# Attention with memory and a gated MoE on one Trainium2 core: the first two blocks as whole float32 stages with z as a column of M, and the first batches' statistics as squares on ACT

## The chip, the cores and the metric

One core of a Trainium2 chip runs the kernel. The metric is device time in microseconds (us), the median of several runs. The kernel before takes 677.45 us (three runs, 676.85 to 678.27).

The engines are named as in the profile: PE (matrix products; PEld is its weight load), DVE (vector), ACT (activations), POOL (GpSimd) and SP, which here only issues DMAs. ACT and POOL can issue DMAs too. Every engine takes its instructions in order.

## The reference

```python
# attention: B, H, S, D = 4, 8, 576, 64
scores = matmul(q, k.T) / sqrt(D), causal
local  = softmax(scores) @ v                 # sum + 1e-9
q_p    = where(q > 0, q, exp(q) - 1) + 1     # phi
mem    = (q_p @ M_prev) / (q_p @ z_prev + 1e-6)
x      = sigmoid(beta) * mem + (1 - sigmoid(beta)) * local
# MoE: 2304 tokens, d_model 512, d_ff 1536, weights float64
xn  = x / sqrt(mean(x * x) + 1e-6) * rms_g
g   = xn @ w_gate
out = (g * sigmoid(g) * (xn @ w_val)) @ w_out
```

## The kernel before

**Blocks and chunks.** The 2304 tokens are 18 blocks of 128 rows, and two blocks make a chunk of 256 tokens, which goes through the MoE together. Blocks 0 and 1 are the first 128 rows of batches 0 and 1. They and chunk 0 are computed in float32. All other blocks split each operand into two float16 parts, a high and a low one, with a power-of-two scale per batch. That scale comes from statistics of the whole batch (the largest norms of k, v and M), so no block after the first two can start before its batch's rows have all been looked at.

**Weights.** They arrive as float64 words in pieces of 512 KB: 24 pieces of `w_gate` and `w_val` (three thirds of eight) and 12 of `w_out`. `f64_to_f32` (L777 to L781) turns a piece into float32 in three steps, one on ACT and two on DVE. Raw pieces lie in a ring of five places in the tile `wo`; a load also waits until the conversion three pieces before it has begun (`PACE`, `paced`). For the later chunks' scales PE forms column sums of the converted pieces (`gram`, L147): four 128x128 products each, whose diagonal bounds the squares.

**Statistics of batches 0 and 1.** `stat_blk` (L232) does the same on the rows of k and v: grams of the four blocks and the tail, tiles `kv` or `pre`, 48 and 32 products. Blocks 2 and 3 of each batch, which are needed in SBUF only later, are loaded for this alone by `load_pre` (L752) into the one buffer of tag `res`, over SP's queue. DVE reduces the sums, with a factor of 1.03. `stat_M` squares M on ACT (`square_acc`, L222).

**Blocks 0 and 1.** k, q and phi(q) are transposed on PE and copied out of PSUM by DVE (L355). Scores, exponentials (L474 on ACT), transposed probabilities, products with v and M go in units of four heads. The sum q_p @ z is a matmul with one column per head (`zn`, L558). M of both batches lies in places of `wo`. The result is squared (L225), its norm is formed on POOL, and a product with a diagonal (L691) gives `xT0`, chunk 0's input. Chunk 0's twelve projections F0 to F11 (L851, float32, sixteen records each) then need all pieces of their third, and its output products (L911) the pieces of `w_out`.

**Order.** The program is a list of steps with estimated lengths and priorities (`PRIO`); a scheduler that simulates the engines lays them into one order per engine. Order on SP's queue matters most, since a load that waits holds up all that stand behind it.

```python
raws[p] = hold(p, 2 * (p % NR))                                        # L746
ins = nc.sync.dma_start(out=raws[p].bitcast(I64), in_=w[...])          # L747
begun[p] = nc.scalar.activation(dst, r[:, :, 1], AF.Prelu, ...)        # L777
nc.vector.tensor_scalar(ri[:, :, 0], ri[:, :, 0], 29, ...)             # L778
nc.vector.scalar_tensor_tensor(out=di, in0=di, scalar=3, ...)          # L779
```

Of the kernel before, what the change touches and what calls it, by code (L numbers as in the profile page):

```python
# [30 lines left out]
ADD32 = "p"  # L31
DIAG = True
T32 = "ddddd"
# [17 lines left out]
RING = 5  # L51
# [7 lines left out]
def attn_memory_moe_kernel(  # L59
# [134 lines left out]
    pre, held = {}, {}  # L194
# [12 lines left out]
    def load_M(b):  # L207
        if b < 2:
            held["M", b, 0] = held["M", b, 1] = NF - b + 100
            qst[("M", b)] = wo[:, NF - b, :]  # L210
        else:
            qst[("M", b)] = sb.tile([P, HD], F32, tag="q", name=f"M{b}")
        for hf in range(2):
            nc.sync.dma_start(
                out=qst[("M", b)][hf * D : (hf + 1) * D], in_=M_prev[b].rearrange("d h e -> d (h e)")
            )
# [5 lines left out]
    def square_acc(src, acc):  # L222
        junk = sb.tile([P, HD], BF16, tag="junk", name="junk", bufs=1)
        np_ = src.shape[0]
        nc.scalar.activation(junk[:np_, : src.shape[1]], src, AF.Square, accum_out=acc)  # L225
# [6 lines left out]
    def stat_blk(b, i):  # L232
        if b < 2:
            r = slice(0, P) if i < NI else slice(b * TR, b * TR + TR)
            src = pre.pop((b, i)) if (b, i) in pre else stage[blk_of[(b, i)] if i < NI else NI * 2]
            for j in range(2):
                if i == 0:
                    csum["kv", b, j] = ps.tile([P, 512], F32, tag="out", name=f"csum{j}")
                gram(csum["kv", b, j], src[r, j], i == 0, i == NI)
                if i == NI:  # L240
                    nc.vector.tensor_reduce(
                        stt[b][:, j, 0:1], csum.pop(("kv", b, j))[:, :P], axis=AX.X, op=ALU.max
                    )
            return
# [9 lines left out]
    def stat_M(b):  # L254
# [6 lines left out]
        del held["M", b, 0]  # L261

    def stat_end(b):
# [6 lines left out]
        if b < 2:  # L270
            nc.vector.tensor_scalar(mx[:, :2], over_partitions(mx[:, :2], 2), 1.03, None, op0=ALU.mult)
            pow2_scales(mx[:, :2], 2, c[:, 0:2], c[:, 3:5])
# [14 lines left out]
    def prep_M(b):  # L287
        src = (qst.pop if b >= 2 else qst.get)(("M", b)).rearrange("p (h e) -> p h e", h=H)
# [23 lines left out]
    def q_stats(n):  # L312
        ss = tiny.tile([P, 2], F32, tag="ss", name="ss")
# [81 lines left out]

    def u_scores(n, h0):
        b, i = blocks[n]
        G = group(n)
        tag = "P16" if n < NA and h0 // G % 2 else "S"
        s = sb.tile([P, NI * P + P], F32, tag=tag, name="S")  # L400
# [5 lines left out]
        for g in range(G):  # L406
            h = h0 + g
            if n < NA:
                h, r = head32(h)
                for j in range(i + 1):  # L410
                    nc.tensor.matmul(
                        t[:, g * w + j * P : g * w + (j + 1) * P], q32[n][r, 0, h // 2, :],
                        k32[blk_of[(b, j)]][r, h // 2, :], start=True, stop=True,
                    )
            elif i < NI:
# [7 lines left out]
        for g in range(G):  # L423
            nc.vector.tensor_tensor_reduce(  # L424
                out=s[:, g * w : (g + 1) * w], in0=t[:, g * w : (g + 1) * w],
                in1=mask[:, m0 : m0 + w], scale=qsc[n][:, 5:6] if n >= NA else -1.0 / float(D) ** 0.5,
# [4 lines left out]
        if n >= NA:  # L431
            nc.vector.tensor_scalar(nm0, nm0, LNP, None, op0=ALU.add)  # L432
# [33 lines left out]
    def u_exp(n, h0):  # L466
        s, w, nm = Ssb[(n, h0)]
        G = group(n)
        if n < NA:
            if h0 % 4 == 0:  # L470
                den[n, h0 // 4] = tiny.tile([P, 2, 4], F32, tag="qsc", name="den", bufs=5)
            for g in range(G):
                v_ = s[:, g * w : (g + 1) * w]
                nc.scalar.activation(  # L474
                    v_, v_, AF.Exp, bias=nm[:, g : g + 1], scale=-1.0,
                    accum_out=den[n, h0 // 4][:, 1, (h0 + g) % 4 : (h0 + g) % 4 + 1],
                )
            Ssb[(n, h0)] = s
            return
# [789 lines left out]
```

## Time and profile before

| what | before |
|---|---|
| median of 3 runs | 677.45 us (676.85 to 678.27) |
| profiled execution, its span | 677.3 us |
| instructions | 16070 |
| PE busy | 623.5 us (92%) |
| PEld busy | 489.4 us (72%) |
| DVE busy | 474.8 us (70%) |
| ACT busy | 384.1 us (57%) |
| POOL busy | 164.3 us (24%) |
| mean granted TensorE clock | 0.944 of full speed |
| moved by DMA | 88.63 MB, 131 GB/s in the mean |

The profiled execution's own time is its span, 677.3 us. A share of busy time is a mean over the whole span; the stages at the start have other limits than the rest, and the rows further down are of those stages. The granted clock is the speed that PE was given, 1.00 being 2.4 GHz and 0.50 being 1.2 GHz.

### The profile page before, as it was taken

What the parts mean: (1) busy time and instruction counts of PE and PEld (TensorE: products, weight loads), DVE (VectorE), ACT (ScalarE), POOL (GpSimd) and SP (SyncE); (2) the same over time, 40 slices, a digit from 0 to 9 for tenths busy, and PEclk for the clock granted to TensorE, in tenths of its full rate; (3) what the DMA queues carried; (4) which work ended last, traced back from release to release, by engine and by line L of the source; (5) the groups of instructions that cost most, each with busy time, mean ns of one, the idle gap of its engine ahead of it and who ended that gap; (6) DMA issues with size and microseconds to landing.
All of it is one profiled execution on the core that took longest, in us unless ns stands there. A gap on an engine that the chain in (4) does not pass through costs nothing.

```text
span 677.3 us, 16070 instructions
## 1 busy us (share of the span) xinstructions
PE 623.5 (92%) x6152; PEld 489.4 (72%) x6152; DVE 474.8 (70%) x1448; ACT 384.1 (57%) x799; POOL 164.3 (24%) x239
## 2 busy tenths in 40 slices
PE   5898968899798969999899899989999999999997
PEld 4786857755686647778687777767787788887774
DVE  5556977897899776689668666877887676872221
ACT  3334655647778776665657656956557554542322
POOL 0001110131255324232143122522232221212111
PEclk9655988899999969999899999999999999999999
DMA  7745899933933777636466763285785454351001
GB/s 257 271 165 198 253 273 249 208 72 63 226 76 76 170 161 167 142 76 146 112 139 111 167 161 64 51 153 135 124 135 114 90 93 99 76 76 21 32 1 31
DMA packets 191660, 88.63 MB, mean 131 GB/s; under 512 B 174176, under 2 KB 174176, under 8 KB 191584
## 3 DMA queue, kind: packets, MB, share of 16 engines
q1 hardware_dynamic: 191136, 87.59, 56.2%
q8 instruction: 48, 0.79, 0.5%
q14 instruction: 28, 0.23, 0.1%
q10 hardware_dynamic: 448, 0.02, 0.0%
HBM read 36.20 MB, written 4.72 MB: 60 GB/s over the span
## 4 chain that ended last, share of the span: by engine, by line
PE 56%; DMA 19%; DVE 11%; ACT 7%; issue 4%; SPq 2%; POOL 1%; ACTq 0%; DVEq 0%; POOLq 0%
PE gv L858 26%; DMA PT<-P 6%; PE out L920 4%; PE out L921 4%; PE out L919 4%; DMA wo<-in_moe_w_out_dram 3%; DMA kv<-in_qkv_dram 3%; PE sc L418 3%; PE sc L445 2%; ACT junk L225 2%; DVE S L424 2%; DMA wo<-in_moe_w_gate_dram 2%; DMA qT<-row 2%; DVE P L500 1%; DMA wo<-in_moe_w_val_dram 1%
## 5 line engine op out<-in xcount | busy, mean ns | idle before, releaser
L858 PE MATMUL gv<-xT,wgv 128*128 128x256 f16 x2304 | 314.5, 274 | 1.3 <-DMA xT<-x 1.3
L858 PEld LDWEIGHTS <-wgv 128*128 128x128 f16 x2304 | 221.9, 98 | 38.4 <-DMA xT<-x 1.5
L890 POOL TENSOR_TENSOR h<-th,h 128x256 f16<-128x256 f32 x96 | 72.4, 754 | 263.1 <-ACT h L889 202.8
L482 ACT ACTIVATE S<-S,nm 128x256 f32<-128x256 f32 (+4 forms) x128 | 75.1, 608 | 47.9 <-DVE nm L432 34.6
L418 PE MATMUL sc<-kT,qT 128*128 128x128 f16 x608 | 84.1, 221 | 4.5 <-DMA qT<-qT 1.8
L500 DVE TENSOR_TENSOR P<-S,P 128x512 f16<-128x512 f32 (+2 forms) x84 | 64.6, 769 | 26.3 <-ACT P L487 25.7
L874 ACT ACTIVATE th<-gv,wt 128x256 f32<-128x256 f32 x96 | 44.8, 467 | 57.4 <-PE gv L858 53.4
L875 DVE SCALAR_TENSOR_TENSOR th<-th,gv 128x256 f32<-128x256 f32 x96 | 39.9, 415 | 52.7 <-ACT th L874 52.1
L424 DVE CUSTOM_DVE_ANT_0 S<-sc,mask,qsc 128x256 f32<-128x256 f32 (+3 forms) x112 | 62.2, 573 | 17.6 <-PE sc L418 14.1
L920 PE MATMUL out<-wo,h 128*128 128x512 f16 x192 | 73.2, 382 | 0.4 <-DVE wo L98 0.4
L921 PE MATMUL out<-wo,h 128*128 128x512 f16 x192 | 72.3, 381 | 0.0
L919 PE MATMUL out<-wo,h 128*128 128x512 f16 x192 | 72.1, 382 | 0.0
L487 ACT CAST P<-S 128x512 f16<-128x512 f32 (+2 forms) x100 | 59.6, 596 | 12.1 <-DMA PT<-P 10.8
L526 PE MATMUL loc<-v,PT 128*128 128x65 f16 x304 | 50.2, 195 | 14.3 <-DMA PT<-P 14.1
L889 ACT CAST h<-th 128x256 f16<-128x256 f32 x96 | 38.4, 400 | 43.9 <-DVE th L878 42.0
L418 PEld LDWEIGHTS <-qT 128*128 128x128 f16 x608 | 51.2, 98 | 10.6 <-issue 3.4
L851 PE MATMUL gv<-xT,wgv 128*128 128x256 f32 x192 | 47.8, 405 | 6.0 <-DVE h32e L878 6.0
L527 PE MATMUL loc<-v,PT 128*128 128x64 f16 x304 | 50.0, 195 | 0.0
L528 PE MATMUL loc<-v,PT 128*128 128x65 f16 x304 | 50.0, 195 | 0.0
L878 DVE SCALAR_TENSOR_TENSOR th<-th,wt,gv 128x256 f32<-128x256 f32 x96 | 45.8, 477 | 1.7
L660 POOL TENSOR_TENSOR t<-t,t 128x256 f32<-128x256 f32 x32 | 25.8, 806 | 86.0 <-DVE t L656 73.5
L851 PEld LDWEIGHTS gv<-xT,wgv 128*128 128x128 f32 x192 | 37.7, 202 | 12.3 <-DVE h32e L878 6.4
(216 smaller groups left out, 1141.5 us busy)
## 6 DMA issues: line engine op xcount, KB each, us to landing
kv<-in_qkv_dram SPq DMA_DIRECT2D x36, 256.0 KB, 3.6
wo<-in_moe_w_gate_dram SPq DMA_DIRECT2D x12, 512.0 KB, 5.5
wo<-in_moe_w_val_dram SPq DMA_DIRECT2D x12, 512.0 KB, 5.3
q<-in_qkv_dram SPq DMA_DIRECT2D x18, 256.0 KB, 3.0
wo<-in_moe_w_out_dram SPq DMA_DIRECT2D x8, 512.0 KB, 4.6
qT<-qT SPq DMA_DIRECT2D x32, 128.0 KB, 2.4
out_dram<-res SPq DMA_DIRECT2D x16, 256.0 KB, 2.3
pre<-in_qkv_dram SPq DMA_DIRECT2D x8, 256.0 KB, 3.0
```

Of the source, the lines that this page charges most:

```text
L418: nc.tensor.matmul(t[:, g * w + j * P : g * w + (j + 1) * P], qT[n][:, t2, h, :], kT[blk_of[(b, j)]][:, h, :], start=(t2 == 0), stop=(t2 = ...
L424: nc.vector.tensor_tensor_reduce(out=s[:, g * w : (g + 1) * w], in0=t[:, g * w : (g + 1) * w], in1=mask[:, m0 : m0 + w], scale=qsc[n][:, 5 ...
L482: nc.scalar.activation(v_, v_, AF.Exp, bias=nm[:, g : g + 1], scale=-1.0)
L487: nc.scalar.copy(p16[:, : G * w], s[:, : G * w])
L500: eng.tensor_tensor(p16[:, w : 2 * w], s[:, :w], p16[:, :w], ALU.subtract)
L526: nc.tensor.matmul(a, phi_, vhi, start=(j == 0), stop=False)
L851: nc.tensor.matmul(o, wgv[:, 1 + p, o0 : o0 + P], xT[0][:, cc, :], start=(cc == 0), stop=(cc == NC - 1))
L858: nc.tensor.matmul(o, lhs, xT[c][:, rhs, :], start=(cnt == 0), stop=(cnt == 3 * NC - 1))
L890: nc.gpsimd.tensor_tensor(h16[:, 1], th, h16[:, 0], ALU.subtract)
L919: nc.tensor.matmul(o, hh, whi, start=(f == 0), stop=False)
L920: nc.tensor.matmul(o, hh, wlo, start=False, stop=False)
L921: nc.tensor.matmul(o, hl, whi, start=False, stop=(f == NF - 1))
```

## The change

1. Blocks 0 and 1 are written as whole stages `scores32`, `mem32`, `pv32` and `evac32`, ahead of the list of steps and at high priority, each over all eight heads. M of batches 0 and 1 lies in tiles `Mz` of tag `v16`, with z as a 65th column, so that one product per head gives both; the `zn` products go. Of ten PSUM copies per pair (`T32`) four go to ACT; the addition of the two halves (`ADD32`) goes from POOL to DVE.
2. The statistics of batches 0 and 1 are squares on ACT (20 of up to 512 columns). The grams on `kv` and `pre`, their reductions and the factor 1.03 go. The eight `pre` loads are issued on POOL's queue (`PREQ`), each into a place of its own of tag `v16`.
3. The ring of raw pieces has six places in place of five; `kv2`, `kv3` and the tail's `kv` are loaded in one row after block 1's inputs; z's scale is a step of its own, `setup_z`.

```diff
-ADD32 = "p"
+ADD32 = "d"
-T32 = "ddddd"
+T32 = "dadda"
-RING = 5
+RING = 6
+PREQ = "p"
...
     def load_M(b):
         if b < 2:
-            held["M", b, 0] = held["M", b, 1] = NF - b + 100
-            qst[("M", b)] = wo[:, NF - b, :]
+            t = sb.tile([P, H, VW], F16, tag="v16", name=f"Mz{b}", bufs=10)
+            Mz[b] = t.bitcast(F32)
+            qst[("M", b)] = Mz[b][:, :, :D]
...
+        if b < 2:
+            nc.gpsimd.tensor_copy(Mz[b][:, :, D], zz[:, b * H : (b + 1) * H])
...
     def stat_blk(b, i):
-        if b < 2:
-            r = slice(0, P) if i < NI else slice(b * TR, b * TR + TR)
-            src = pre.pop((b, i)) if (b, i) in pre else stage[blk_of[(b, i)] if i < NI else NI * 2]
-            for j in range(2):
-                if i == 0:
-                    csum["kv", b, j] = ps.tile([P, 512], F32, tag="out", name=f"csum{j}")
-                gram(csum["kv", b, j], src[r, j], i == 0, i == NI)
...
+        if (b, i) in pre:
+            for j, src in enumerate(pre.pop((b, i))):
+                square_acc(src, stt[b][:, j, i : i + 1])
             return
...
+    def mem32(n):
+        b = blocks[n][0]
+        accs[n] = [ps.tile([P, 4, D + 1], F32, tag="out", name=f"mem{n}_{u}") for u in range(2)]
+        for g in range(4):
+            for u in range(2):
+                h, r = head32(4 * u + g)
+                nc.tensor.matmul(
+                    accs[n][u][:, g], q32[n][r, 1, h // 2, :], Mz[b][r, h, :], start=True, stop=True
+                )
...
-    def mem32(n, g4):
-        b, i = blocks[n]
-        if g4 == 0:
-            z = ps.tile([P, 2, 4], F32, tag="sc", name="zn")
-            for x in range(H):
-                h, r = head32(x)
...
-                nc.tensor.matmul(
-                    zt[:, x // 4, x % 4 : x % 4 + 1], q32[n][r, 1, h // 2, :],
-                    zz[r, b * H + h : b * H + h + 1], start=True, stop=True,
-                )
...
     def load_pre(b, i):
-        pre[(b, i)] = sb.tile([P, 2, HD], F32, tag="res", name=f"pre{b}_{i}", bufs=1)
+        pre[(b, i)] = []
         for j in range(2):
-            nc.sync.dma_start(out=pre[(b, i)][:, j], in_=qkv[blk_of[(b, i)], :, j, :])
+            t = sb.tile([P, H, VW], F16, tag="v16", name=f"pre{b}_{i}_{j}", bufs=10)
+            t = t.bitcast(F32).rearrange("p a b -> p (a b)")[:, :HD]
+            PRE.dma_start(out=t, in_=qkv[blk_of[(b, i)], :, j, :])
+            pre[(b, i)].append(t)
...
-    load_kv(2), load_kv(3)
     setup_consts()
-    for n in range(2):
-        prep_qk32(n)
-        phi_calc(n)
-        prep_phi32(n)
+    with tc.high_priority(PRIO[0]):
+        for n in range(2):
+            prep_qk32(n)
+            phi_calc(n)
+            scores32(n)
+            prep_phi32(n)
+            mem32(n)
+        for n in range(2):
+            pv32(n)
+            evac32(n)
+            x_norm(n)
+            x_float(n)
     load_q(2)
+    load_kv(2), load_kv(3), load_kv(2 * NI)
+    for i in range(2, NI):
+        for b in range(2):
+            load_pre(b, i)
+    with tc.high_priority(PRIO[0]):
+        setup_z()
```

What that does to the order of instructions stands below at three places. A row is line, operation, out<-in and shape; `x4` is four such in a row, and the numbers in names count tiles.

On SP's queue, after the inputs of block 1, the kernel before has

```order
L220 DMA q2_188<-in_qkv_dram 128x512
L747 DMA wo_84<-in_moe_w_gate_dram 128x512
L747 DMA wo_84<-in_moe_w_val_dram 128x512
L220 DMA q3_766<-in_qkv_dram 128x512
L747 DMA wo_84<-in_moe_w_val_dram 128x512
L756 DMA pre0_3_529<-in_qkv_dram 128x512 x2
L747 DMA wo_84<-in_moe_w_val_dram 128x512 x2
L747 DMA wo_84<-in_moe_w_gate_dram 128x512
L756 DMA pre1_2_635<-in_qkv_dram 128x512 x2
L747 DMA wo_84<-in_moe_w_gate_dram 128x512 x3
L756 DMA pre1_3_646<-in_qkv_dram 128x512 x2
L747 DMA wo_84<-in_moe_w_val_dram 128x512 x4
```

and the changed kernel, whose weight loads are at L739,

```order
L224 DMA q2_343<-in_qkv_dram 128x512
L206 DMA kv2_345<-in_qkv_dram 128x512 x2
L206 DMA kv3_348<-in_qkv_dram 128x512 x2
L206 DMA kv8_351<-in_qkv_dram 128x512 x2
L739 DMA wo_84<-in_moe_w_gate_dram 128x512
L739 DMA wo_84<-in_moe_w_val_dram 128x512
L224 DMA q3_603<-in_qkv_dram 128x512
L739 DMA wo_84<-in_moe_w_val_dram 128x512 x3
L739 DMA wo_84<-in_moe_w_gate_dram 128x512 x4
L739 DMA wo_84<-in_moe_w_val_dram 128x512 x4
L739 DMA wo_84<-in_moe_w_gate_dram 128x512 x4
L739 DMA wo_84<-in_moe_w_val_dram 128x512 x3
```

The `pre` loads are gone from among the weight loads; `kv2`, `kv3` and the tail `kv8` stand ahead of the fourth weight piece.

On ACT, from the square of block 0's result (`t1_0`; `wgv<-wo` is a conversion, `ph` a step of phi, `ssm` belongs to M's statistics, `ss` to q's), the kernel before has

```order
L225 ACTIVATE junk_326,xs_325<-t1_0_289 128x512
L777 ACTIVATE wgv_83<-wo_84 128x512 x5
L225 ACTIVATE junk_388,xs_387<-t1_1_374 128x512
L335 ACTIVATE ph_738<-q2_188 128x512
L777 ACTIVATE wgv_83<-wo_84 128x512
L225 ACTIVATE junk_471,ssm0_470<-wo_84 128x512
L777 ACTIVATE wgv_83<-wo_84 128x512 x2
L225 ACTIVATE junk_594,ssm1_593<-wo_84 128x512
L225 ACTIVATE junk_709,ss_708<-q2_188 128x512
L777 ACTIVATE wgv_83<-wo_84 128x512
```

and the changed kernel, from the square of block 1's result, with `stt` for the statistics of k and v and conversions at L771,

```order
L233 ACTIVATE junk_331,xs_330<-t1_1_324 128x512
L233 ACTIVATE junk_371,zq_370<-zz_86 128x32
L771 ACTIVATE wgv_83<-wo_84 128x512 x2
L233 ACTIVATE junk_466,ssm0_465<-Mz0_101 128x512
L233 ACTIVATE junk_492,stt0_490<-kv0_98 128x512
L771 ACTIVATE wgv_83<-wo_84 128x512
L233 ACTIVATE junk_494,stt0_490<-kv0_98 128x512
L771 ACTIVATE wgv_83<-wo_84 128x512
L233 ACTIVATE junk_496,stt0_490<-kv2_345 128x512
L233 ACTIVATE junk_498,stt0_490<-kv2_345 128x512
L771 ACTIVATE wgv_83<-wo_84 128x512
L96 ACTIVATE zhl_87<-zz_86,zs_88 128x32
```

Squares of k and v stand between the conversions, and the first square of a `pre` tile comes soon after this piece.

On PE, just ahead of F6, which is `gv_927` before and `gv_857` in the changed kernel (`wo` rows are column sums of output pieces, `PT` rows products of block 2's probabilities with v), the kernel before has

```order
L147 LDWEIGHTS wo
L147 MATMUL csum<-wo 128x128
L147 LDWEIGHTS wgv
L147 MATMUL csum<-wgv 128x128
L147 LDWEIGHTS wgv
L147 MATMUL csum<-wgv 128x128
L851 MATMUL gv_927<-xT_330,wgv 128x256 x8
L418 LDWEIGHTS qT_727
```

and the changed kernel

```order
L577 LDWEIGHTS PT
L577 MATMUL loc_0_834<-v_2_598,PT 128x64
L578 LDWEIGHTS PT
L578 MATMUL loc_0_834<-v_2_598,PT 128x65
L148 LDWEIGHTS wo
L148 MATMUL csum<-wo 128x128
...
L148 LDWEIGHTS wo
L148 MATMUL csum<-wo 128x128
L845 MATMUL gv_857<-xT_288,wgv 128x256 x8
L845 MATMUL gv_985<-xT_288,wgv 128x256 x3
```

Ahead of F6 stand in all 12 products on `wo`, those of three output pieces, before, and 32, those of eight, in the changed kernel; F7 follows at once there.

## Rows read from the trace of the kernel before

**Rows 1.** Busy time by stretch: stretch, length, each engine's busy us (instructions), clock, DMA, GB/s.

```profile
0.00:17.00 17.00, 8.65 (x60) 7.52 (x60) 8.93 (x45) 5.25 (x12) 1.37 (x13) 1.00 0.80 258
16.00:20.00 4.00, 1.64 (x15) 1.29 (x12) 4.00 (x20) 3.58 (x17) 0.00 (x0) 1.00 1.03 310
24.00:64.00 40.00, 37.06 (x185) 32.28 (x185) 21.02 (x63) 11.96 (x34) 4.86 (x10) 0.50 0.51 172
64.00:82.00 18.00, 18.00 (x116) 14.28 (x116) 16.25 (x54) 11.73 (x23) 0.11 (x1) 0.94 0.85 282
82.00:136.00 54.00, 43.69 (x340) 37.41 (x339) 43.12 (x129) 33.66 (x65) 8.48 (x12) 0.87 1.03 237
```

**Rows 2.** Waits of SP's queue, 0 to 135 us: total, times, longest.

```profile
SPq L747 <- ACT wgv L777: 16.6, 10, 3.7
SPq L756 <- PE csum L147: 13.9, 2, 7.9
SPq L756 <- PE tp L351: 7.7, 1, 7.7
```

**Rows 3.** Waits of ACT, 24 to 64 us.

```profile
ACT S L474 <- DVE nm L424: 12.1, 2, 6.9
```

**Rows 4.** The chain in time, first and last of its weight pieces: start, length, what.

```profile
67.16 4.49 DMA wo<-in_moe_w_gate_dram
...
95.47 7.05 DMA wo<-in_moe_w_out_dram
```

**Rows 5.** Timeline of PE: projections and the first output matmul.

```profile
67.50 0.70 PE L851 MATMUL gv<-xT,wgv 128*128 128x256 f32 x2
...
103.88 5.28 PE L851 MATMUL gv<-xT,wgv 128*128 128x256 f32 x16 [5.81 <-DVE h32e L878]
110.67 3.70 PE L851 MATMUL gv<-xT,wgv 128*128 128x256 f32 x16
...
127.18 5.36 PE L851 MATMUL gv<-xT,wgv 128*128 128x256 f32 x16
...
143.90 7.13 PE L911 MATMUL out<-wo,h32e 128*128 128x512 f32 x16
```

**Rows 6.** Waits of PE from 143.9 us to the end, the largest.

```profile
PE loc L526 <- DMA PT<-P: 11.8, 11, 2.1
```

**Rows 7.** Groups of instructions, 0 to 135 us: busy, mean ns, idle before.

```profile
L147 PE MATMUL csum<-kv 128*128 128x128 bf16 (+1 forms) x48 | 6.8, 298 | 2.5 <-DMA kv<-in_qkv_dram 2.5
L147 PE MATMUL csum<-pre 128*128 128x128 bf16 x32 | 4.7, 295 | 0.9 <-DMA pre<-in_qkv_dram 0.9
L147 PE MATMUL csum<-wo 128*128 128x128 bf16 x36 | 3.5, 228 | 2.0 <-DVE wo L779 1.9
L558 PE MATMUL zn<-zz,q 64*128 64x1 f32 x32 | 7.9, 344 | 0.0
L778 DVE TENSOR_SCALAR wo<-wo 128x512 int32<-128x512 int32 x32 | 13.6, 426 | 10.3 <-DMA wo<-in_moe_w_out_dram 8.2 <-DMA wo<-in_moe_w_gate_dram 1.5 <-DMA wo<-in_moe_w_val_dram 0.4
L779 DVE SCALAR_TENSOR_TENSOR wgv<-wgv,wo 128x512 int32<-128x512 int32 x24 | 17.5, 728 | 0.9 <-ACT wgv L777 0.4
```

**Rows 8.** Timeline of ACT: conversions (L777), squares (L225) and what is near.

```profile
29.13 1.20 ACT L777 ACTIVATE wgv<-wo 128x512 f32<-128x512 f32 x2
...
39.02 0.63 ACT L225 ACTIVATE junk<-t 128x512 bf16<-128x512 f32 x1 [1.28 <-POOL t L600]
...
60.20 0.63 ACT L225 ACTIVATE junk<-t 128x512 bf16<-128x512 f32 x1 [6.92 <-POOL t L600]
...
83.25 0.65 ACT L777 ACTIVATE wgv<-wo 128x512 f32<-128x512 f32 x1
...
113.32 0.70 ACT L777 ACTIVATE wo<-wo 128x512 f32<-128x512 f32 x1 [0.64 <-DMA wo<-in_moe_w_out_dram]
```

**Rows 9.** DMA issues of the page: count, KB each, us to landing.

```profile
wo<-in_moe_w_gate_dram SPq DMA_DIRECT2D x12, 512.0 KB, 5.5
...
pre<-in_qkv_dram SPq DMA_DIRECT2D x8, 256.0 KB, 3.0
```

More of the change, by code (lines that the diff above doesn't have):

```diff
@@ new lines, in mem32, with pv32 @@
+    def mem32(n):
+        b = blocks[n][0]
+        accs[n] = [ps.tile([P, 4, D + 1], F32, tag="out", name=f"mem{n}_{u}") for u in range(2)]
+        for g in range(4):
+            for u in range(2):
+                h, r = head32(4 * u + g)
+                nc.tensor.matmul(
+                    accs[n][u][:, g], q32[n][r, 1, h // 2, :], Mz[b][r, h, :], start=True, stop=True
+                )
+    def pv32(n):
+        loc = ps.tile([P, H, D], F32, tag=f"a{n}", name=f"loc{n}", bufs=1)
+        for u in range(2):
+            pt = sb.tile([P, NC, P], F32, tag="PT", name="PT32", bufs=LAG + 1)
+            transposed(pt, Ssb[n][u], T32[3 + u] == "a")
+            for g in range(4):
+                h = head32(4 * u + g)[0]
+                nc.tensor.matmul(
+                    loc[:, 4 * u + g], pt[:, g, :], stage[n][:, 1, h * D : h * D + D],
+                    start=True, stop=True,
+                )
+        accs[n].append(loc)
+        Ssb.pop(n)
@@ L407, in u_scores @@
             h = h0 + g
-            if n < NA:
-                h, r = head32(h)
-                for j in range(i + 1):
-                    nc.tensor.matmul(
[L412 to L415, printed above, removed]
+            if i < NI:
                 for j in range(i + 1):
@@ L468, in u_exp @@
         G = group(n)
[L469 to L479, printed above, removed]
         for g in range(G):
@@ L762, in load_wo @@
         else:
-            assert at < 11 or not any(x[0] == "M" for x in held if type(x) is tuple)
             r = hold(("o", f), at)
@@ L961, in attn_memory_moe_kernel @@
     marks = {}
-    units = [(n, h0) for n in range(NBLK) for h0 in range(0, H, group(n))]
+    units = [(n, h0) for n in range(NA, NBLK) for h0 in range(0, H, group(n))]
     def prep_steps(n):
@@ L1039, in attn_memory_moe_kernel @@
             load_w(*pcs[p])
-    load_kv(2), load_kv(3)
     setup_consts()
-    for n in range(2):
-        prep_qk32(n)
-        phi_calc(n)
-        prep_phi32(n)
-    load_q(2)
-    STATS = {NA - 2: 0, NA - 1: 1}
+    with tc.high_priority(PRIO[0]):
[10 more added lines that the diff above has]
+            x_float(n)
+    load_q(2)
+    load_kv(2), load_kv(3), load_kv(2 * NI)
[4 more added lines that the diff above has]
+        setup_z()
+    for b in range(2):
+        a(NA + b, 0.7, stat_M, b)
+        a(NA + b, 2.0, all_stats, b)
+        late_prep(b)
+        if b == 0:
+            for x in prep_steps(NA):
+                for w, fn in x:
+                    a(NA, w, fn)
     tails = [n for n in range(NBLK) if is_tail[n]]
```

175 lines of the change are left out of this document (76 added, 99 removed).

## Prediction

> **What bounds the kernel now.** I read the page first: TensorE (PE) is busy 92% of the span, so a gain has to come either from PE work that disappears or from a stretch in which PE is not what sets the pace. The table of busy time by stretch shows where that is [rows 1]. Up to 17 us the loads run at 258 GB/s. From 24 to 64 us PE is busy 37.06 of 40 us, but at a granted clock of 0.50 (its lower level), while the DMA engines move 172 GB/s, ACT works 11.96 us and DVE 21.02. From 64 to 82 us the loads run at 282 GB/s and DVE is busy 16.25 of 18 us; from 82 to 136 us the DMA share is 1.03 at 237 GB/s. So weights that could have come in 24 to 64 us come afterwards. The waits of SP's queue say why [rows 2]: the `pre` loads (L756) stand 13.9 us behind PE's column sums and 7.7 us behind its transposes, with weight loads behind them in the same queue, and 16.6 us go to weight loads that wait for the conversion three pieces earlier. ACT is in the same knot: it waits 12.1 us for block 0/1's scores [rows 3] and 1.28 and 6.92 us for their results [rows 8], with pieces to convert queued behind. The chain in time [rows 4] then goes from weight piece to weight piece, so the late pieces are what counts.
>
> What they delay is on PE [rows 5]: the first projection starts at 67.50 us, the seventh (F6) at 103.88, after 5.81 us of idle, and the first output matmul ("out start") at 143.90. The rows of PE from there on (8048 of 11289) stand in the same order in both kernels, and PE waits little in them: 11.8 us on its largest item [rows 6]. Hence the rest, 677.3 - 143.9 = 533.4 us, is taken as fixed, and the question is when out start comes.
>
> **The parts.** PE loses the `kv` and `pre` column sums, 6.8 + 4.7 us, and the `zn` matmuls, 7.9 us [rows 7]: 19.4 us of PE, at the low clock, all ahead of or between the steps of blocks 0 and 1. These run now as whole stages ahead of the rest. That alone is worth nothing at the end, since the weights set it; its worth is that ACT and SP no longer stand behind PE. I follow ACT.
>
> (A) *When ACT gets free.* Before, the square of block 0's result is at 39.02 us and block 1's at 60.20 [rows 8]. In the changed order block 0's square comes after all sixteen exponentials, and then conversions, block 1's square and the statistics follow in one row. The inputs of both blocks stand at the head of SP's queue, ahead of the third weight piece. With that piece the queue holds about 4.4 MB, which the 258 GB/s of [rows 1] bring in 17 us; 11 us of DVE and PE steps of the kind seen between 17 and 29 us remain: 28 us. Bounds: 24 (nothing is late) and 36 (the two blocks' DVE steps stay in series).
>
> The 2.1 MB of `pre` loads now compete in that time from POOL's queue. In the trace of before the `pre` loads go over SP's queue, as all large loads do [rows 9], so their price on another is bounded: nothing if POOL's queue adds bandwidth, and 2.1 MB / 0.31 = 7 us if the 310 GB/s of 16 to 20 us [rows 1] are all there is. I take the second for the weights, but charge only 1 us of it to block 0, whose inputs are ahead; the rest is inside (B). The Trainium skill (DMA: Bandwidth & Descriptors, section Issuing engines are not separate DMA queues) says that DMAs of all issuing engines share the same 16 engines and another queue only saves issue time; by it the 7 us hold, without it w3 would be there 7 us earlier. No run here shows it yet.
>
> (B) *To the 24th conversion.* From block 0's square to the 24th conversion the changed order gives ACT 20 conversions of 0.60, 22 squares of 0.63 [rows 8], 10 casts of the same width, taken at 0.63 too, and some 2.3 us of small ones: 34.5 us. DVE has about as much: 20 x (0.43 + 0.73) for the two other steps of a conversion [rows 7] and some 11 us beside. How dense can ACT run? DVE reached 90% in 64 to 82 us, ACT 33.66/54 = 62% in 82 to 136 [rows 1]. I take 85%, nearer the first, because the inputs are in SBUF by then: 40.5 us, so 68.5. The loads give a second floor: until then SP and POOL bring 24 pieces of 512 KB (12.6 MB) [rows 9] and 6.3 MB of `q`, `k`, `v` and M, `pre` among them, 18.9 MB, at 282 GB/s 67 us. Two limits so close never both run full: +3, **71.5 us**, against 83.25 before [rows 8].
>
> (C) *The output pieces.* In the changed PE order F6 stands behind the column sums of 8 output pieces; before, behind 3. So I need the eighth. Before, it is converted at 113.32 us, 30.1 after the 24th [rows 8]. Between the two SP carried about 6.3 MB and 5 transposes; now 5.5 MB and 2, the others having moved ahead: 30.1 x 5.5/6.3 = 26. Bounds 21 (5.5 MB at 258 GB/s) and 30.1. So 97.5; the conversion's rest and the sums take 0.70 + 0.43 + 0.73 + 4 x 0.23 = 2.8 [rows 7, 8], and F6 starts at **100.3 us**, against 103.88.
>
> (D) *F6 to out start.* 40.0 us before. Two of the six projections took 5.28 and 5.36 us instead of 3.70 [rows 5], 3.2 us; and DVE waits 8.2 us in all for output pieces [rows 7], most of which are now there by F6. I take 36; bounds 40 (nothing gained) and 32. Out start **136.3 us**.
>
> (E) 136.3 + 533.4 = 669.7 us for the profiled execution, whose 677.3 us lie 0.15 below the median of 677.45: **670** rounded. Of 19.4 us of PE work taken out, under 8 are seen at the end.
>
> At nothing I cost the z column (one column more per matmul, under cover of the loads), the casts of M, the PSUM copies that move to ACT (4, each the size of a conversion, ahead of block 0's square, while loads run), POOL's addition that goes to DVE, the deeper ring (each load still waits for the conversion three pieces earlier), and POOL's issues, which end before it is asked for the norms at 28 us. If a load did not land until then, each would cost its own length.
>
> **Rivals.**
> *ACT becomes the bound and the late sums gate PE: slower.* 20 squares are new on ACT, and F6 waits for five more pieces. If ACT runs at its 62%, 34.5 us become 55.4, the 24th conversion is at 83.4, the eighth piece at 113.5, F6 at 116.3, out start at 152.3: 685.7 us. It decides if the eighth output piece is converted later than 143.9 - 36 - 2.8 = 105.1 us. For it: no stretch of [rows 1] shows ACT above 65%, apart from 16 to 20 us. Against: its idle there is waiting [rows 3] that is removed. Chance 0.14.
>
> *POOL's loads come late.* The first `pre` square stands about 10 us behind block 0's square, near 38 us, and ACT runs in order. If these loads land at 50 instead, 12 us are lost, of which the 6 us of idle in (B) absorb half: 676 us, and with it the change is nearly nothing. For it: DVE is busy half of the time [rows 1], and no POOL load is in the trace; against: SP's `pre` loads take 3.0 us from issue to landing [rows 9], and these are issued some 20 us ahead. The Trainium skill (SBUF — State Buffer, section SBUF: two separate sides) states the mechanism: a DMA from GpSimd's queue has its descriptors written by GpSimd, which is kept off the shared port while DVE runs a two-port operation. No row here shows it. Chance 0.06.
>
> *The output pieces are late anyway: no change.* At a density of 75% and without (C)'s saving, the 24th conversion is at 74, the eighth piece at 104.1, out start at 142.9: 676.4. Chance 0.10 with all that ends within the bound of no change, 0.2% or 1.35 us, about what a measurement of this kernel can tell.
>
> *More than forecast.* The loads alone set (B), 67 us, (C) is 21 and (D) 32: out start 122.8, or 656.3 us. Chance 0.08.
>
> **How the numbers follow.** The forecast's own case, out start between 123 and 141 us, has 0.62. With it the last rival is faster, and 0.06 of the 0.16 of the two that end near nothing: 0.76. Of these two 0.09 are same and 0.01 slower: with the first rival 0.15. The likeliest time is 670. The range leaves out about 0.07 below and 0.13 above: 656 to 679. The forecast's own range is 656.5 to 674.5.
>
> **What would show it.** In the profile after: block 0's square near 28 us and the first projection near 40 (67.50 before); no wait of SP for column sums; ACT some 85% busy from 28 to 69 us; the 24th conversion near 71, the eighth output piece near 97, F6 near 100 and out start near 136. It is wrong in (A) if the POOL loads show landings after 38 us, in (B) if ACT has long waits in that stretch, in (C) if F6 starts long after the eighth piece, and in (E) if out start to end is not 533 us.

## The result, and the profile after

The changed kernel takes 662.52 us (four runs, 659.53 to 663.35) against 677.86 us for the kernel before beside it: a ratio of 0.9761, 95% interval 0.9733 to 0.9789; the medians are 15.3 us apart. Forecast were 670 us and a range of 656 to 679. The time lies in the range and on the side that was forecast, but the gain is twice the forecast one, and the milestones show that it did not come from where the prediction looked for it. That the time lies in the range is luck: out start, on which the forecast rested, came at 142.05 us instead of 136.3, and with the prediction's own remainder of 533.4 us that would have been 675.5 us.

The page of the changed kernel, its first lines and the DMA issue that is new:

```profile
span 661.2 us, 15900 instructions
...
PE 601.0 (91%) x6040; PEld 469.2 (71%) x6040; DVE 470.3 (71%) x1438; ACT 394.6 (60%) x843; POOL 166.5 (25%) x245
...
pre<-in_qkv_dram POOLq DMA_DIRECT2D x8, 256.0 KB, 7.2
```

Busy time by stretch, with the columns of [rows 1]; the last line is the stretch from the first output matmul to where M of batch 2 is loaded:

```profile
0.00:17.00 17.00, 9.05 (x54) 7.82 (x55) 10.25 (x42) 8.12 (x24) 6.03 (x18) 1.00 0.84 265
24.00:64.00 40.00, 36.23 (x192) 29.30 (x190) 30.54 (x97) 28.24 (x79) 3.35 (x11) 0.87 0.75 253
64.00:82.00 18.00, 7.81 (x24) 6.48 (x25) 13.63 (x42) 15.07 (x32) 2.77 (x3) 0.62 0.90 249
82.00:136.00 54.00, 40.63 (x363) 33.88 (x363) 41.55 (x142) 29.59 (x59) 6.25 (x11) 0.87 0.85 206
142.05:257.30 115.25, 106.63 (x1036) 76.33 (x1037) 97.90 (x299) 87.29 (x179) 42.35 (x52) 1.00 0.69 136
```

From 24 to 64 us the picture is the forecast one: ACT 28.24 us of work instead of 11.96, loads at 253 GB/s instead of 172, and PE at a granted clock of 0.87 instead of 0.50.

The milestones on ACT, in its timeline: block 0's square, batch 0's first cast with its scale (`row<-kv,cb`), the 24th conversion, the eighth output piece. They answer to [rows 8]:

```profile
32.89 0.64 ACT L233 ACTIVATE junk<-t 128x512 bf16<-128x512 f32 x1
...
66.00 0.71 ACT L96 ACTIVATE row<-kv,cb 128x512 f16<-128x512 f32 x1
...
75.45 0.69 ACT L771 ACTIVATE wgv<-wo 128x512 f32<-128x512 f32 x1 [0.62 <-DMA wo<-in_moe_w_val_dram]
...
102.65 0.66 ACT L771 ACTIVATE wo<-wo 128x512 f32<-128x512 f32 x1
```

And on PE, F6 and out start, which answer to [rows 5]:

```profile
106.05 7.00 PE L845 MATMUL gv<-xT,wgv 128*128 128x256 f32 x22
...
142.05 7.13 PE L905 MATMUL out<-wo,h32e 128*128 128x512 f32 x16 [0.94 <-DVE wmx L813]
```

F6 starts 2.2 us later than before and out start only 1.85 us earlier, yet the span is 16.1 us shorter. So 14.25 us of the gain lie behind out start, where the prediction had put none. Most of it is in the stretch from out start to the load of M of batch 2. In the kernel before that stretch is the first row here, and the second is 10 us of it:

```profile
143.90:270.50 126.60, 111.11 (x1041) 79.11 (x1041) 101.43 (x320) 90.60 (x182) 44.81 (x53) 0.95 0.58 129
240.00:250.00 10.00, 4.36 (x73) 3.54 (x70) 5.93 (x18) 8.91 (x20) 3.74 (x5) 0.68 0.72 166
```

The stretch between the same two marks takes 126.60 us before and 115.25 after, 11.35 of the 14.25 us: PE idles 15.5 us instead of 8.6, and is busy for 111.1 instead of 106.6 us at a mean granted clock of 0.95 instead of 1.00; from 240 to 250 us, where PE is busy for 4.36 us, it is 0.68. Around that gap chunk 1's output is finished (240.7 and 242.7 us), and chunk 2's first projection waits for block 5's result:

```profile
249.97 4.23 PE L858 MATMUL gv<-xT,wgv 128*128 128x256 f16 x20 [1.35 <-DMA xT<-x]
```

The transposition of block 5's result on SP's queue, before and after:

```profile
246.12 1.53 SPq L708 DMA_TRANSPOSE xT<-x  x1
```

```profile
234.44 1.24 SPq L699 DMA_TRANSPOSE xT<-x  x1
```

It comes 11.7 us earlier, and batch 0's first cast 13.5 us earlier (79.53 before). The other 4.4 us of the span's 16.1 lie behind block 5's result, and no run explains them. The two earlier milestones suggest **theory A**: the end follows the time at which the scales of batches 0 and 1 let the attention of blocks 2 to 5 begin. **Theory B**: the end follows the PE work that is taken out (19.4 us). **Theory C**, the prediction's: it follows out start.

### The profile page after: what moved, and what is told of

It is laid out like the page before. It is cut to its first block, busy times and chain, and to the rows that moved or that the text cites. A ratio compares the mean times of both kernels' runs of the same rounds, so it can differ in the third digit from the quotient of the medians.

```text
span 661.2 us, 15900 instructions
## 1 busy us (share of the span) xinstructions
PE 601.0 (91%) x6040; PEld 469.2 (71%) x6040; DVE 470.3 (71%) x1438; ACT 394.6 (60%) x843; POOL 166.5 (25%) x245
## 4 chain that ended last, share of the span: by engine, by line
PE 54%; DMA 19%; DVE 13%; ACT 7%; issue 4%; POOL 2%; SPq 1%; ACTq 0%; POOLq 0%; DVEq 0%
PE gv L852 24%; DMA PT<-P 6%; PE out L914 4%; PE out L915 4%; PE out L913 4%; PE gv L845 4%; DMA wo<-in_moe_w_out_dram 3%; DMA xT<-x 3%; PE sc L486 3%; DMA qT<-row 3%; DVE S L492 2%; PE sc L512 2%; DMA kv<-in_qkv_dram 2%; ACT junk L233 2%; DVE P L552 1%
## 5 line engine op out<-in xcount | busy, mean ns | idle before, releaser
L552 DVE TENSOR_TENSOR P<-S,P 128x512 f16<-128x512 f32 (+2 forms) x84 | 63.5, 757 | 29.2 <-ACT P L543 28.7
L492 DVE CUSTOM_DVE_ANT_0 S<-sc,mask,qsc 128x256 f32<-128x256 f32 (+3 forms) x112 | 62.2, 573 | 16.3 <-PE sc L486 10.4
L845 PE MATMUL gv<-xT,wgv 128*128 128x256 f32 x192 | 51.8, 429 | 10.4 <-DVE h32e L872 10.4
L845 PEld LDWEIGHTS gv<-xT,wgv 128*128 128x128 f32 x192 | 40.2, 216 | 18.2 <-DVE h32e L872 10.5
L576 PEld LDWEIGHTS <-PT 128*128 128x128 f16 x304 | 29.2, 98 | 22.5 <-DMA PT<-P 17.9
```

The lines of the kernel that those rows point to most:

```text
L492: nc.vector.tensor_tensor_reduce(out=s[:, g * w : (g + 1) * w], in0=t[:, g * w : (g + 1) * w], in1=mask[:, m0 : m0 + w], scale=qsc[n][:, 5:6],
L552: eng.tensor_tensor(p16[:, w : 2 * w], s[:, :w], p16[:, :w], ALU.subtract)
L576: nc.tensor.matmul(a, phi_, vhi, start=(j == 0), stop=False)
L845: nc.tensor.matmul(o, wgv[:, 1 + p, o0 : o0 + P], xT[0][:, cc, :], start=(cc == 0), stop=(cc == NC - 1))
```

## The experiments

All times are medians, each with the ratio to the kernel before beside it on the same chip. The executions of one kernel lie mostly within 1.5% of each other, so a few us between runs of different chips say little; the milestones, of one profiled execution each, say where the time goes.

**e1_delay.** The scales delayed by an idle chain on POOL, nothing else:

```diff
         nc.vector.tensor_reduce(mx, stt[b], axis=AX.X, op=ALU.max)
+        if b < 2:
+            for _ in range(70):
+                nc.gpsimd.tensor_scalar(mx, mx, 1.0, None, op0=ALU.mult)
```

> The changed kernel (662.5 us), with 70 tiny POOL operations put into the path of the statistics of batch 0 and of batch 1, so that k's and v's scales come about 14 us later; nothing else moves on purpose, the result is the same. Theory A (the scales' time decides: blocks 2 to 5 of attention start when they are there, and when block 5 is done decides when chunk 2 can start): 672 to 679 us, with the gap of PE near 240 to 250 us of the kernel before back. Theory B (PE's relief from 19.4 us of products is what is gained): 662 to 665 us. Theory C (the first output matmul decides, as in the prediction): it moves little, since it waits for output pieces, so 662 to 666 us.

685.92 us, ratio 1.0109 (1.004 to 1.0178). The delay became 22 us, not 14: the first cast is at 88.23 and it now waits for the scale. The whole gain is gone and more (theory A said 672 to 679), with PE still relieved of its 19.4 us and the output pieces earlier than in the changed kernel (eighth at 91.3 us). B falls, and early pieces do not help by themselves. Out start moved too, to 159.2, so C is not told apart here. The gap that theory A expected near 240 to 250 us did not come back: chunk 1 was late as well, its output is finished at 262.7 and 265.2 us, behind block 5's result.

```profile
88.23 0.72 ACT L96 ACTIVATE row<-kv,cb 128x512 f16<-128x512 f32 x1 [3.77 <-DVE cb L277]
```

```profile
254.73 1.24 SPq L702 DMA_TRANSPOSE xT<-x  x1
```

**e2_grams.** Squares undone, places and POOL's queue kept:

```diff
-            for j, src in enumerate(pre.pop((b, i))):
-                square_acc(src, stt[b][:, j, i : i + 1])
...
+            for j in range(2):
...
+                gram(csum["kv", b, j], src[j][r], i == 0, i == NI)
```

> The changed kernel with the statistics of batches 0 and 1 as column sums on PE again (80 products, 11.5 us of PE in the trace before; factor 1.03 back), the pre loads left on POOL's queue in places of their own, blocks 0 and 1 as whole stages. Theory A: PE has its inputs early, so the scales come within 5 us of the changed kernel's and the time is 660 to 668 us. Theory B: PE's 11.5 us come back, 668 to 674 us.

662.63 us, ratio 0.979 (0.9716 to 0.9864). The 11.5 us of PE work are back and cost nothing. Out start comes 12.8 us earlier than in the changed kernel, block 5's result 2.7 us earlier, and the span is 2 us shorter. That speaks against C, and against B as e1 does:

```profile
129.28 1.98 PE L915 MATMUL out<-wo,h32e 128*128 128x512 f32 x4 [0.38 <-DVE wmx L823]
```

```profile
231.77 1.24 SPq L709 DMA_TRANSPOSE xT<-x  x1
```

**e3_squares.** The kernel before with `stat_blk`, `load_pre` and the `kv` loads of the change, blocks 0 and 1 untouched:

```diff
...
+        if (b, i) in pre:
+            for j, src in enumerate(pre.pop((b, i))):
+                square_acc(src, stt[b][:, j, i : i + 1])
```

> The kernel before (677.9 us), with only the statistics changed: squares on ACT, pre loads on POOL's queue into places of their own, kv loads early in a row; blocks 0 and 1 as before with their 32 zn products. Theory A: the scales come earlier by what SP's waits on column sums had cost, and the time falls with the first score product of block 2, one for one: 665 to 672 us. Theory B: PE is relieved of 11.5 of the 19.4 us, 667 to 669 us. Theory C: the time moves as the first output matmul does.

688.97 us, ratio 1.0158 (1.0055 to 1.0261): slower than before. On ACT the squares stand behind the square of block 1's result, which still waits for the blocks' own slow chain, and the first cast comes at 84.37 us:

```profile
59.84 0.63 ACT L225 ACTIVATE junk<-t 128x512 bf16<-128x512 f32 x1 [7.24 <-POOL t L591]
...
84.37 0.71 ACT L95 ACTIVATE row<-kv,cb 128x512 f16<-128x512 f32 x1
```

Theories A and B expected a gain; A's rule (late cast, late end) held, its guess about the cast did not. Out start is late by 10.3 us too (154.2), so C's rule fits this run as well.

**e4_sp.** `PREQ = "s"`: the `pre` loads on SP's queue.

> The changed kernel with the eight pre loads on SP's queue instead of POOL's, ahead of the fourth weight piece. If all queues share the same bandwidth and SP only loses the issue time: 661 to 665 us. If POOL's queue brings bandwidth of its own, the weight pieces behind the 2.1 MB come up to 7 us later: 664 to 669 us.

659.95 us, ratio 0.9757 (0.9679 to 0.9836): no slower, so the 664 to 669 us that bandwidth of its own on POOL's queue would have meant are not seen. The third weight piece, which stands ahead of the `pre` loads on SP's queue, is converted at 16.18 us; in the changed kernel the 2.1 MB from POOL go beside it, and ACT and DVE wait for it until 22.55. The DMA share is 1.05 from 16 to 24 us in both, with 347 GB/s in the changed kernel and 402 here, so POOL's queue adds no bandwidth. The same shows over all runs with whole stages and block 1's inputs behind the first two pieces: with POOL's queue in use the third piece is waited for until 22.1 to 22.6 us in six profiles (18.1 and 19.1 in two, e12 and e1); on SP's queue it is converted at 16.2 to 18.4 us in six.

**e5_zn.** z out of the M product again:

```diff
-                nc.tensor.matmul(
-                    accs[n][u][:, g], q32[n][r, 1, h // 2, :], Mz[b][r, h, :], start=True, stop=True
...
+                for e0, e1 in ((0, D), (D, D + 1)):
+                    nc.tensor.matmul(
+                        accs[n][u][:, g, e0:e1], q32[n][r, 1, h // 2, :], Mz[b][r, h, e0:e1],
...
```

> The changed kernel with z taken out of the M product again: 16 products of 64 columns and 16 of one column in place of 16 of 65, so PE's part of the removed zn work (7.9 us in the trace before, at the low clock) is back inside the whole stages. Theory A (time of the first cast with batch 0's scales, 66 us in the changed kernel, plus 592 to 606 us is the end): the stages wait for loads until 24 us anyway, so the cast moves by under 3 us and the time stays within 660 to 666 us. Theory B (relief of PE): 4 to 8 us more, 666 to 671 us.

676.5 us, ratio 0.9958 (0.9927 to 0.999): 16 small products cost 14 us, more than either theory gave. PE's own time grows little: block 1's M products take 3.60 us instead of 1.97. The trace shows another loss. The scheduler now puts the third piece's conversion ahead of block 1's k copy on DVE, and the piece has not landed; PE waits for the copy. DVE, then PE:

```profile
22.11 0.43 DVE L774 TENSOR_SCALAR wo<-wo 128x512 int32<-128x512 int32 x1 [6.47 <-DMA wo<-in_moe_w_gate_dram]
```

```profile
25.31 0.90 PE L349 MATMUL tp<-ident,ph 128*128 128x128 f32 x3 [8.81 <-DVE k L353]
```

Block 0's square comes at 44.4 us (32.9), the first cast at 79.1 (66.0), and the end with it.

**e6_stages_only.** The first part of the change, with the ring of six places and the early `kv` loads of the third: e2's sums, and `load_pre` on SP into the one `res` buffer as before.

> The first part of the change alone: whole stages and the z column, but the statistics as column sums on PE and the pre loads in the one buffer of tag res on SP's queue as in the kernel before, so that SP again waits for PE between weight loads. Theory A: the column sums have no blocks 0 and 1 ahead of them any more, SP waits less than the 21.6 us of before, the first cast comes within 8 us of 66 and the time is 660 to 670 us. Rival D (SP's waits on the pre loads are what cost): the weights come as late as before and the time is 672 to 678 us.

671.11 us, ratio 0.9896 (0.9864 to 0.9928). SP still waits for column sums, but 4.4 us instead of the 13.9 of [rows 2]; the cast is at 71.1. The time lies between the ranges of theory A (660 to 670) and rival D (672 to 678). So the stages, with ring and `kv` loads, give half of the gain.

**e7_small.** `T32 = "ddddd"`, `ADD32 = "p"`, `RING = 5` in the changed kernel.

> The changed kernel with its small switches as before: PSUM copies all on DVE, the addition of the two halves on POOL, a ring of five raw pieces. Theory A: these lie in blocks 0/1's chain; block 1's square and with it the scales come 1 to 4 us later, 662 to 667 us. Rival: the ring of six carries the loads, without it 667 to 672 us.

667.84 us, ratio 0.9828 (0.976 to 0.9896), with executions from 662.1 to 670.0. The cast is at 72.0. The median lies in the rival's range (667 to 672, the ring of six), the executions in both; the third piece was late here too (22.59 us). So neither is settled.

**e8_hybrid.** Batch 0 by squares, batch 1 by column sums, `pre` on SP:

```diff
+GB = 1
...
+        if b == GB:
+            r = slice(0, P) if i < NI else slice(b * TR, b * TR + TR)
...
```

> The changed kernel with batch 0's statistics as squares on ACT and batch 1's as column sums on PE, and the pre loads on SP's queue: ACT has 10 squares (6.3 us) less in the stretch from 40 to 78 us, where it is 82 to 98% busy, and PE, which is nearly idle from 64 to 75 us, takes them. Theory A: batch 0's first cast comes some 3 to 6 us earlier and the end follows: 653 to 660 us, faster than the changed kernel. Theories B and C: no gain, 660 to 668 us.

662.88 us, ratio 0.9789 (0.971 to 0.9868): no gain, against A's guess. The cast is only 1.6 us earlier (64.4), though out start is at 126.5; chunk 1's output is finished at 224.3 us, and PE is busy for 5.68 of the 10 us from 220 on, before block 5 is done at 229.95.

**e9_zn_sp.** e5_zn with `PREQ = "s"`.

> The kernel of e5_zn (16 products of one column for z back) with the pre loads on SP's queue. In e5_zn block 1's k copy stood on DVE behind a step of the third weight piece, which waited for its landing at 22.1 us, since the 2.1 MB on POOL's queue shared the bandwidth. Theory A with that reading: the third piece lands near 17 us as in e4_sp, blocks 0 and 1 are done some 10 us earlier than in e5_zn, and the time is 660 to 667 us. Theory B (z's products cost PE the time): it stays at 673 to 678 us.

674.33 us, ratio 0.9929 (0.9896 to 0.9962): in theory B's range, so the reading of e5_zn was at least incomplete. The third piece is there at 16.9 us, but the next conversions stand ahead of block 1's steps on DVE as well, and the weights' column sums ahead of its products on PE, which wait for that DVE step with the rest behind them:

```profile
34.08 1.14 PE L148 MATMUL csum<-wgv 128*128 128x128 bf16 x9 [6.03 <-DVE t L464]
```

**e10_own_places.** The kernel before with the loads of the change alone (places of their own on POOL's queue, `kv` early), column sums and old blocks.

> The kernel before with the loads of the change alone: pre loads on POOL's queue into places of their own and the kv loads early in a row; statistics as column sums on PE and blocks 0 and 1 as before. If SP's 21.6 us of waits for PE behind the pre loads were what held the scales back (rival D): 662 to 669 us. Theory A: PE has blocks 0 and 1 and the sums to do at the low clock until 60 us as before, the first cast comes within 4 us of 79.5, 674 to 682 us.

679.95 us, ratio 1.0019 (0.9986 to 1.0052): nothing, though SP's waits for column sums and transposes behind the `pre` loads, 21.6 us before [rows 2], are gone. The cast is at 78.4. Rival D falls; the weight loads now wait 21.0 us for ACT's conversions and 14.0 us for DVE's. Together with the stages the places do count (e2 against e6: 662.6 and 671.1).

**e11_inputs_first.** e4_sp with `HORD = "q0 k0 M0 q1 k1 M1 w0 w1"`.

> A try for more: the changed kernel with the pre loads on SP's queue and block 1's q, k, v and M ahead of the first weight pieces, so that no DVE step of blocks 0 and 1 stands behind a piece that has not landed. Theory A: block 1's square and the first cast come 2 to 6 us earlier than in e4_sp (62.2 us), 654 to 660 us. Rival: in the changed kernel PE and DVE are already 90% busy while blocks 2 to 5 run, so an earlier cast gives nothing: 659 to 663 us.

664.72 us, ratio 0.9786 (0.9728 to 0.9843): slower than the changed kernel beside it (e12, 655.94) and than both ranges expected. Blocks 0 and 1 are squared at 33.7 and 38.6 us (29.2 and 32.3 in e4_sp), and the cast is at 72.0, 9.8 us later than there; yet block 5 is only 1.8 us later. So the cast alone does not tell when block 5 is done.

**e12_after_again** and **e14_after_third**, the changed kernel on two other chips.

> The changed kernel itself, on the same chip as the other three of this call: 658 to 666 us.

> The changed kernel itself, on the same chip as the others of this call: 655 to 664 us.

655.94 us (expected 658 to 666), ratio 0.968 (0.9628 to 0.9732), and 663.57 us, ratio 0.977 (0.9709 to 0.9831). The profiled executions differ by 9 us (654.0 and 663.1) with the same instructions. They part first where DVE waits for the third piece: 18.07 us in e12, 22.6 in e14 and 22.55 in the first profile.

```profile
18.07 0.43 DVE L772 TENSOR_SCALAR wo<-wo 128x512 int32<-128x512 int32 x1 [0.58 <-DMA wo<-in_moe_w_gate_dram]
```

```profile
22.55 0.43 DVE L772 TENSOR_SCALAR wo<-wo 128x512 int32<-128x512 int32 x1 [5.42 <-DMA wo<-in_moe_w_gate_dram]
```

The casts of e12 and e14 are at 62.4 and 67.7 us, block 5's result at 229.3 and 236.9. So 4.5 us of one landing go with 7 us at the end (first profile, 661.2) and 9 us (e14); how they grow is not shown, and in e14 PE's granted clock was also 0.50 from 16 to 40 us, against 1.00 (to 24 us) and 0.95 (behind it) in the first profile.

**e13_late_products.** e5_zn's 16 products, but behind the results of blocks 0 and 1:

```diff
+        for _ in range(H):
+            nc.tensor.matmul(t[:, 0, 0:1], x[:, :P], ident[:, 0:1], start=True, stop=True)
```

> The changed kernel with the same 16 one-column float32 products added that e5_zn and e9_zn_sp had put back, but after block 0's and block 1's results (on the result tile, their output overwritten), so that the order of DVE's steps for blocks 0 and 1 stays that of the changed kernel; SP's and POOL's orders are word for word the same. Theory A (e5_zn and e9_zn_sp were slow since the conversions of weight pieces moved ahead of blocks 0/1's steps on DVE and PE's order followed): within 3 us of the changed kernel on this chip. Theory B (the products' PE time): 8 us or more above it, as e5_zn and e9_zn_sp were by 14 and 18.

Inconclusive: its median is 670.31 us, 6.7 above e14's and so between the two theories, but three of its four executions lie at 670.09 to 672.39 us and one at 659.99, within e14's 656.21 to 664.83. The profiled one (672.39) has the cast at 69.2 us, 1.5 after e14's, where e5_zn had it 13 us late. So the products alone move the cast little, but what they cost at the end is not settled.

**e15_grams_sp.** e2_grams with `PREQ = "s"`.

> Whole stages, column sums on PE and the pre loads on SP's queue in places of their own, so neither squares nor POOL's queue: what is left of the change when its second part is only the places. Theory A: the first cast within 3 us of the changed kernel's, and the time within 5 us of it. Theory that squares matter: 8 us or more above it.

656.65 us, ratio 0.9709 (0.9686 to 0.9733), 7 us below the changed kernel on its chip (e14), where theory A allowed 5. Neither squares nor POOL's queue is needed; the third piece is converted at 16.6 us. The cast comes 0.4 us later than e14's, block 5's result 8.4 us earlier.

**e16_early_squares.** `PREQ = "s"`, and the first k and v squares of both batches taken at once:

```diff
     def all_stats(b):
-        stat_begin(b)
-        for i in range(NI + 1):
+        for i in range(1, NI + 1):
...
     with tc.high_priority(PRIO[0]):
         setup_z()
+        for b in range(2):
+            stat_begin(b)
+            stat_blk(b, 0)
```

> A try for more: the changed kernel with the pre loads on SP's queue and the squares of the first k and v blocks of both batches taken at once at high priority, ahead of the other statistics. Theory A: batch 1's scales come some 2 us earlier, batch 0's no earlier, the time is within 4 us of the changed kernel's, rather below.

651.89 us, ratio 0.9624 (0.9587 to 0.966), the fastest kernel of this study; its interval lies below that of the changed kernel on the same chip (0.9709 to 0.9831). It is 11.7 us below e14, where theory A expected to be within 4. Block 2's first score product starts at 69.38 us (82.88 in the changed kernel, 97.12 before) and block 5 is done at 223.5:

```profile
69.38 0.39 PE L486 MATMUL sc<-kT,qT 128*128 128x128 f16 x2 [1.57 <-DMA qT<-row]
```

```profile
223.52 1.30 SPq L699 DMA_TRANSPOSE xT<-x  x1
```

The cast is where e4_sp has it (62.5 and 62.2 us), so the 11 us between their first score products (e4_sp: 80.49) are not the scales' doing. The order on PE is: in the changed kernel projections of chunk 0, which wait for DVE, stand ahead of block 2's first score product; in e16 the product stands ahead of them and waits for its operand alone. The changed kernel:

```profile
74.19 2.08 PE L845 MATMUL gv<-xT,wgv 128*128 128x256 f32 x4 [10.42 <-DVE h32e L872]
...
82.88 0.28 PE L486 MATMUL sc<-kT,qT 128*128 128x128 f16 x2
```

e4_sp, e5, e7, e8 and e9 have the order of the changed kernel there; e2, e6, e11 and e15 have that of e16.

**The profiled executions together** (without e13), in us (first cast with batch 0's scales, transposition of block 5's result, out start):

| run | span | cast | block 5 | out start | span - block 5 | span - out start |
|---|---|---|---|---|---|---|
| before | 677.3 | 79.5 | 246.1 | 143.9 | 431.2 | 533.4 |
| after | 661.2 | 66.0 | 234.4 | 142.1 | 426.8 | 519.2 |
| e1_delay | 680.4 | 88.2 | 254.7 | 159.2 | 425.7 | 521.2 |
| e2_grams | 659.2 | 67.4 | 231.8 | 129.3 | 427.4 | 529.9 |
| e3_squares | 690.1 | 84.4 | 257.4 | 154.2 | 432.7 | 535.9 |
| e4_sp | 659.0 | 62.2 | 231.5 | 136.9 | 427.5 | 522.1 |
| e5_zn | 678.5 | 79.1 | 243.3 | 145.7 | 435.2 | 532.9 |
| e6_stages_only | 670.9 | 71.1 | 240.5 | 136.7 | 430.4 | 534.2 |
| e7_small | 668.2 | 72.0 | 240.7 | 143.5 | 427.5 | 524.7 |
| e8_hybrid | 660.3 | 64.4 | 230.0 | 126.5 | 430.3 | 533.8 |
| e9_zn_sp | 673.8 | 76.3 | 240.9 | 142.4 | 432.9 | 531.4 |
| e10_own_places | 678.8 | 78.4 | 246.3 | 146.3 | 432.5 | 532.5 |
| e11_inputs_first | 665.1 | 72.0 | 233.3 | 133.0 | 431.8 | 532.1 |
| e12_after_again | 654.0 | 62.4 | 229.3 | 136.7 | 424.7 | 517.3 |
| e14_after_third | 663.1 | 67.7 | 236.9 | 143.5 | 426.2 | 519.6 |
| e15_grams_sp | 656.7 | 68.2 | 228.5 | 131.3 | 428.2 | 525.4 |
| e16_early_squares | 650.4 | 62.5 | 223.5 | 126.7 | 426.9 | 523.8 |

From block 5's result to the end it is 424.7 to 435.2 us, a spread of 10.5 over spans that differ by 40; from out start the spread is 18.6. The cast's own distance to the end varies by 17.8 (587.9 in e16, 605.7 in e3), so by this alone the cast tells the end no better than out start does. The cast is a cause that was moved by hand, in e1; PE's order ahead of the first score product is probably another (e16 against e4_sp: the cast in one place, block 5 8.0 us earlier), and block 5's result is where they have added up. That block 5's result goes with the end is seen over these runs; it was not moved by itself.

## Why the prediction was wrong

**(E) is the step that failed.** "The rows of PE from there on (8048 of 11289) stand in the same order in both kernels [...] Hence the rest, 677.3 - 143.9 = 533.4 us, is taken as fixed." The remainder was not fixed: it measured 519.2 us, 14.2 less. What was wrong is the place where the common order begins. It is not out start: in the two traces the last 4029 matmuls follow in the same order, by tile names and shapes, and they begin at 294.30 us before and at 279.48 after, behind block 5's result. From there to the end it is 383.0 and 381.7 us:

```profile
294.30:677.30 383.00, 371.10 (x4032) 291.74 (x4028) 254.94 (x759) 207.61 (x433) 94.60 (x139) 1.00 0.47 96
```

```profile
279.48:661.20 381.72, 369.60 (x4032) 290.57 (x4029) 254.45 (x759) 207.04 (x433) 94.54 (x139) 1.00 0.51 96
```

So this part was as good as fixed, and 13.0 of the 16.1 us lie between out start and it (150.4 and 137.4 us). There PE works on chunks 0 and 1 and on attention side by side, and the kernel before had its idle PE and its lowered clock. The prediction did read PE's waits behind out start, but only their largest item [rows 6]: 11.8 us for transposed probabilities, which it called little. The waits of PE in the kernel before from 143.9 to 270.5 us show that nearly all of it lies in this stretch; after, it is 6.2 us from 142 to 257.3:

```profile
PE loc L526 <- DMA PT<-P: 10.9, 10, 2.1
```

```profile
PE loc L576 <- DMA PT<-P: 6.2, 7, 1.3
```

With it falls the prediction's view that the late weight pieces are what counts: in e1 the output pieces came early and the end late, and in e10 SP's waits behind the `pre` loads, to which it put the pieces' delay down, are gone and the time stays.

**(A) to (D) held, as sums.** In the profile after, (A) came at 32.9 us instead of 28, (B) at 75.45 instead of 71.5, (C) at 102.65 instead of 97.5 and F6 at 106.05 instead of 100.3: all late by about the 5 us that (A) lost, 3.8 of them to the third piece, by e12. (B)'s part, from block 0's square to the 24th conversion, took 42.6 us (forecast 43.5), (C)'s 27.2 (26) and (D) 36.0, as forecast; the 3 us that (B) added for two close limits no run shows by itself. In e12, where that piece came at 18 us, the same milestones stand at 29.1, 72.6 and 97.9 us, and out start at 136.7, forecast 136.3; yet the span is 654.0, not 669.7. So the forecast of out start was good, and out start was the wrong thing to forecast. An earlier out start is not the source of the gain: in e2 and e8 it comes 13 to 16 us earlier still and the end moves by 1 to 2 us.

**The 2.1 MB on POOL's queue** were charged with 1 us on block 0; together with the place of the third piece's steps on DVE they go with 3.8 us at block 0's square in two of the three profiles of the changed kernel. The rows show no bandwidth added: the DMA share is 1.05 from 16 to 24 us with POOL's queue in use, and on SP's queue alone (e4) as well. That agrees with the Trainium skill (DMA: Bandwidth & Descriptors, section Issuing engines are not separate DMA queues), by which DMAs of all issuing engines run on the same 16 DMA engines.

**The rivals.** ACT was not the bound at 62%: it was 71% busy from 24 to 64 us and 84% from 64 to 82, against the 85% of the sum. F6 did come later than before, as that rival had it, and it did not matter. POOL's loads were not late: its eight issues took 4.49 us from 8.18 us on, with a median of 7.2 us to landing, and ACT's wait list of 24 to 84 us has none on a `pre` tile. DVE was busy for 3.86 of the 4.49 us of issue. The Trainium skill (SBUF — State Buffer, section SBUF: two separate sides) says that GpSimd cannot write descriptors while DVE runs a two-port operation; no such delay is seen here, but no row says which of DVE's operations were of that kind.

**What gives the gain**, by runs that undo or add a part, on different chips: the stages with the ring and the early `kv` loads 8.5 us (e6); places of their own for the `pre` loads 7 to 13 more by the ratios, but only with the stages (e2 and e15 against e6; e10 alone nothing); squares instead of column sums nothing (e2, e15), and without the stages they cost some 9 (e3 against e10); POOL's queue nothing or a loss (e4, e15). The z column is worth 14 to 18 us in this scheduler's hands (e5 and e9 against the changed kernel): without it weight conversions are placed ahead of blocks 0/1's steps. That the changed order and not PE's time is what costs there is argued from the waits in e5 and e9 and from the 3.60 us against 1.97; it is not proved, since e9 lies where theory B had it and e13 stays open.

## What to carry to other kernels

Before a remainder is called fixed, look up at which row the two orders really become the same, and what is late in the stretch ahead of it. Where two streams of work share an engine, the milestone to forecast is the end of the stream that opens the next stage (here block 5's result), not the first visible output of the other. And an early operand pays only if nothing that still waits, for a load or for another engine, stands in front of its user on any engine: here a projection held block 2's first score product back, long after the scales were there (82.88 us; the cast was at 66.0).

## What was not expected of the hardware

Profiled executions of one program differ by 7 to 9 us where one 512 KB load, issued on SP's queue beside 2.1 MB on POOL's, is waited for until 18.1 us or until 22.6. Two queues at once did not move more than one: from 16 to 24 us 347 GB/s in the first profile, 354 in e14 and 397 in e12, against 402 in e4_sp, at a DMA share of 1.03 to 1.05 in all. And PE's granted clock is no plain matter of being busy: before it stood at 0.50, its lower level, from 24 to 64 us, in which PE was busy for 37.06 us [rows 1], in the changed kernel at 0.87 in the mean with 36.23.
